# Attention: the scores of two key blocks merged by an elementwise maximum, one transpose per head, the two triangles taken apart on GpSimd

## The chip, the cores and the metric

The kernel runs on one core of a Trainium2 chip. The core has TensorE (matrix products, PE in the profile; PEld is its weight load), VectorE (DVE), ScalarE (ACT), GpSimd (POOL), and SyncE (SP), which here issues DMAs. Each engine works through its own instructions in order and waits on semaphores for the others. The metric is the device time of one execution in microseconds; several runs are taken and their median is given.

## The reference

Three stages follow each other: windowed attention, a mixture of 8 experts of which each row takes one, and a weighted sum over 4 experts.

```
B, H, S, D = q.shape                      # 4, 8, 576, 64
window = 128
scores = scale * np.matmul(q, k.transpose(0, 1, 3, 2))
bias = slopes[:, None, None] * (-np.abs(rel))[None, :, :]     # rel = query - key
mask = (rel >= 0) & (rel < window)
scores = np.where(mask, scores + bias[None], -1000000000.0)
scores = scores - np.max(scores, axis=-1, keepdims=True)
attn = np.exp(scores)
attn = attn / (np.sum(attn, axis=-1, keepdims=True) + 1e-09)
x = np.matmul(attn, v)                    # then [2304, 512]
expert_idx = np.argmax(x @ w_gate, axis=1)
...                                       # each row through relu(x @ w1[e]) @ w2[e] of its expert
...                                       # then sum over 4 experts of p[:, e] * relu(x @ w1[e]) @ w2[e]
```

With a window of 128 a block of 128 queries sees two blocks of 128 keys: its own, where key j counts for query i if j <= i, and the one before, where it counts if j > i. The two triangles complete each other.

## The kernel before

The 2304 rows are 18 tiles of 128. The attention stage is a loop over steps `s`; a step is half a tile (`t, hf = divmod(s, 2)`), that is four heads of 128 queries, so there are 36 steps and some more to empty the pipeline. The order of work on each engine is the order in which the loop writes it; nothing is moved by a scheduler. Each engine keeps that order, so an instruction that waits holds all behind it on its engine.

In step `s` the loop writes, in this order:

- `st_qk(s)`: TensorE puts the bias (two products with an identity, L412) and the scores (12 products in three float32r parts, L420) of both key blocks into PSUM tile `sc`, 128 queries x 4 heads x 256 keys. Two such tiles exist.
- `st_max(s)`: VectorE reduces `sc` to the negated row maximum `nm` (L429).
- `st_exp(s, 0)` and later `st_exp(s, 1)`: ScalarE writes the exponentials, 256 wide, for two heads each, from PSUM into `pr` (L437).
- `st_pv(s - 2)`: TensorE multiplies the transposed probabilities of the step before the last with the values (`xo`, L463; the value tile `vr` also holds a column of ones for the sum and 8 columns of the gate product).
- `st_row(s - 2)`: VectorE normalises (`den`, `xrow`, `lgh`); at the end of a tile it sums the gate logits (`lg`).
- in odd steps `st_vw(t)`: TensorE multiplies the values of the tile with the gate weights (`vw`, L523), and VectorE copies that into `vr`.
- `st_pv_t(s - 1, 0)` and `(s - 1, 1)`: TensorE transposes the probabilities, four 128x128 blocks each (`pt`, L448), and ScalarE copies them out (`ptr`, L450).
- loads (`load`, `load_v`, issued by SP), and the splits of keys and queries into a high and a low part (`split_k`, `split_q`, on VectorE: `khi`, `klo`, `qhi`, `qlo`).
- up to five small pieces of `late_consts` on GpSimd, among them the bias tables (`build_bias`, L302).
- in six of the steps (`SPLITS`) the cast of a weight tile of the expert stage on ScalarE (`whi`, L134), and in the step after it its low half on VectorE (`wlo`, L138).

Four times in a step `route_op` takes one piece of the routing. When the logits of a group of tiles (`CUTS`: four groups of three, two of two, two of one; the last two come after the steps) are there, `st_route` makes the one-hot of the best expert on VectorE (`key`, `km`, `oh_all`), then the rank of each row in its expert on TensorE (`rkp`, L574 to L580), then the row numbers on VectorE (`row_i`, `base`), and GpSimd scatters the rows to HBM with one indirect DMA a tile (L606). After the steps `first_chunk` gathers the first rows of expert 0: those of the first 16 tiles come back from HBM (`early`), those of the last two through products with a placement matrix (`xps`); their casts (L185) begin the expert stage.

Tiles 0 and 9 begin a batch and have one key block; the others have two.

Of the kernel before, what the change touches and what calls it, by code (L numbers as in the profile page):

```python
# [9 lines left out]
F32 = mybir.dt.float32  # L10
F32R = mybir.dt.float32r
BF16 = mybir.dt.bfloat16
I32 = mybir.dt.int32
# [4 lines left out]
P = 128  # L18
# [32 lines left out]
def kernel(  # L51
# [153 lines left out]
    def attention():  # L205
        actx = ExitStack()
        with actx:
# [40 lines left out]
            def split_q(t):  # L248
# [3 lines left out]
                nc.vector.tensor_scalar(out=hi, in0=rq, scalar1=0.125, scalar2=None, op0=ALU.mult)  # L252
# [17 lines left out]
            rel_i = spool.tile([P, 2 * P], I32, tag="pr", name="rel_i")  # L270
# [25 lines left out]
            def build_bias(x, h, o, w, eng):  # L296
                slope = 2.0 ** (-8.0 * (h + 1) / H)
                out = biases[x][:, h, o:o + w]
                if eng is nc.scalar:
                    nc.scalar.activation(out=out, in_=rels[x][:, 0:w], func=AF.Copy, scale=-slope)  # L300
                else:
                    eng.tensor_scalar(out=out, in0=rels[x][:, 0:w], scalar1=-slope, scalar2=None, op0=ALU.mult)  # L302

            for h in range(H):
                build_bias(0, h, 0, 2 * P, nc.scalar)
# [14 lines left out]
            def late_consts():  # L320
                for h in range(H):
                    build_bias(0, h, 2 * P, P, nc.gpsimd)
                    yield

                for x in (1, 2):
# [6 lines left out]
                    for h in range(H):  # L332
                        build_bias(x, h, 0, 2 * P, nc.gpsimd)
                        yield
                        if x == 1:
                            build_bias(x, h, 2 * P, P, nc.gpsimd)
                            yield
                tri = c2.tile([P, P], BF16, tag="tri", name="tri")
                trif = c2.tile([P, P], F32, tag="trif", name="trif")
# [31 lines left out]
                slot_i = c2.tile([P, CH], I32, tag="slot_i", name="slot_i")  # L371
# [61 lines left out]
            def st_exp(s, jj):  # L433
                w = len(geom(s // 2)[0]) * P
                pr, nm = prob[s]
                for r in range(2):
# [923 lines left out]
```

## Time and profile before

| | |
|---|---|
| median of 3 runs | 1180.62 us (1180.06 to 1180.85) |
| the profiled execution, in all | 1181.98 us |
| its span | 1180.3 us |
| mean clock granted to TensorE | 0.995 of full speed |
| TensorE busy | 1161.1 us, 98% of the span |
| VectorE busy | 777.9 us, 66% |
| ScalarE busy | 510.6 us, 43% |
| GpSimd busy | 93.9 us, 8% |

The attention stage is the first 182 us or so. A row of the timeline gives the start in us from the span's start, the time from the first start to the last end, the engine, the line, the operation, the tiles (out<-in), the shape, and how many instructions are merged in it; in square brackets stands how long the engine was idle before, and what it waited for. Matmuls are pipelined, so the distance between two starts counts, not the duration.

### The profile page before, as it was taken

The page shows a single profiled execution, that of the slowest core. Times are in us where ns is not written, and L with a number is a line of the kernel's source. Part 1 is how long each engine was busy: PE and PEld are TensorE (multiplying, and loading weights), DVE is VectorE, ACT ScalarE, POOL GpSimd, SP SyncE. Part 2 cuts the span into 40 slices and gives each one's busy share as a digit, 9 for nine tenths or more (in the row PEclk, how much of TensorE's full clock was granted, in tenths as well). Part 3 has the DMA queues.
Part 4 walks back from the last instruction along what each step waited for, and adds up shares of the span by engine and source line. Part 5 has one row for each costly group of instructions (what it writes and reads, how often), then busy time and mean ns, then how long its engine had stood idle before and what let it go on. Part 6 is the DMA issues. An engine that isn't in the chain of part 4 may idle for free.

```text
span 1180.3 us, 18010 instructions
## 1 busy us (share of the span) xinstructions
PE 1161.1 (98%) x6997; PEld 1060.7 (90%) x6998; DVE 777.9 (66%) x1428; ACT 510.6 (43%) x928; POOL 93.9 (8%) x126
## 2 busy tenths in 40 slices
PE   8999999999999999999999999999999999999997
PEld 6888889999999999999999899999999899999996
DVE  6778865564555476666666976666667866666663
ACT  4565654544454353333334444333334533333331
POOL 8300010002310000000000200000000200000001
PEclk8999999999999999999999999999999999999999
DMA  9856434554564322222112322221221322222201
GB/s 310 272 161 199 135 99 163 167 178 153 174 197 133 116 73 72 72 72 70 56 58 70 116 81 72 72 71 58 70 72 59 120 73 72 72 72 72 72 18 54
DMA packets 62225, 126.60 MB, mean 107 GB/s; under 512 B 26272, under 2 KB 26272, under 8 KB 62112
## 3 DMA queue, kind: packets, MB, share of 16 engines
q1 hardware_dynamic: 58368, 114.96, 30.7%
q0 software_dynamic: 3456, 9.51, 2.1%
q8 instruction: 82, 1.34, 0.4%
q10 hardware_dynamic: 288, 0.52, 0.1%
q14 instruction: 31, 0.25, 0.1%
HBM read 109.18 MB, written 15.80 MB: 106 GB/s over the span
## 4 chain that ended last, share of the span: by engine, by line
issue 70%; PE 25%; DVE 2%; POOL 2%; ACT 0%; DMA 0%; POOLq 0%
PE g L766 6%; PE y L871 6%; PE xo L463 5%; PE sc L420 3%; PE pt L448 2%; POOL out_dram L1291 2%; PE vw L523 1%; PE sc L412 1%; PE xps L838 1%; DMA rk<-in_k_dram 0%; DVE nm L429 0%; DVE xrow L493 0%; DVE qlo L253 0%; DVE qhi L252 0%; PE idle L104 0%
## 5 line engine op out<-in xcount | busy, mean ns | idle before, releaser
L138 DVE TENSOR_TENSOR wlo<-raw,whi 128x1024 fp32r<-128x1024 f32 x160 | 193.3, 1221 | 133.4 <-ACT whi L134 133.4
L1270 PE MATMUL l<-whi,hhi 128*128 128x512 f32 x576 | 224.3, 389 | 1.6 <-DVE acc L1287 1.6
L1270 PE MATMUL l<-whi,hlo 128*128 128x512 f32 x576 | 224.6, 390 | 0.0
L1270 PE MATMUL l<-wlo,hhi 128*128 128x512 f32 x576 | 224.5, 390 | 0.0
L134 ACT CAST whi<-raw 128x1024 fp32r<-128x1024 f32 x160 | 165.9, 1057 | 128.6 <-DVE raw L160 104.6
L1187 ACT COPY x<-X 128x384 f32<-128x384 f32 x126 | 60.6, 481 | 270.0 <-PE X L1166 270.0
L1287 DVE SCALAR_TENSOR_TENSOR acc<-l,ct,acc 128x512 f32<-128x512 f32 x126 | 94.1, 747 | 81.7 <-PE l L1270 81.7
L1270 PEld LDWEIGHTS l<-whi,hhi 128*128 128x128 f32 x576 | 108.1, 188 | 24.3 <-DVE acc L1287 2.5
L1270 PEld LDWEIGHTS l<-whi,hlo 128*128 128x128 f32 x576 | 108.1, 188 | 22.5
L1270 PEld LDWEIGHTS l<-wlo,hhi 128*128 128x128 f32 x576 | 108.1, 188 | 22.0
L1192 DVE TENSOR_TENSOR x<-Z,x 128x384 f32<-128x384 f32 x84 | 44.6, 551 | 67.7 <-ACT x L1187 67.7
L1291 POOL DMA_INDIRECT out_dram<-acc,ctok x18 | 22.3, 1238 | 823.4 <-DVE acc L1287 488.2
L437 ACT ACTIVATE pr<-sc,nm 128x256 f32<-128x256 f32 (+1 forms) x144 | 59.0, 465 | 51.0 <-DVE nm L429 22.5
L1198 ACT ACTIVATE hhi<-x 128x384 fp32r<-128x384 f32 x126 | 58.1, 521 | 30.8 <-DVE x L1192 30.8
L871 PE MATMUL y<-hhi,whi 128*128 128x256 f32 (+2 forms) x224 | 69.5, 310 | 1.6 <-issue 1.6
L463 PE MATMUL xo<-vr,ptr 128*128 128x73 f32 x544 | 69.2, 279 | 0.4 <-ACT ptr L450 0.2
L871 PE MATMUL y<-hhi,wlo 128*128 128x256 f32 (+2 forms) x224 | 69.0, 308 | 0.0
L871 PE MATMUL y<-hlo,whi 128*128 128x256 f32 (+2 forms) x224 | 68.8, 307 | 0.0
L463 PEld LDWEIGHTS xo<-vr,ptr 128*128 128x128 f32 x544 | 63.7, 191 | 5.5 <-ACT ptr L450 0.7
L1204 DVE SCALAR_TENSOR_TENSOR hlo<-x,hhi 128x384 fp32r<-128x384 f32 x126 | 62.8, 552 | 2.7
L755 DVE SCALAR_TENSOR_TENSOR hlo<-g,hhi 128x384 fp32r<-128x384 f32 x64 | 32.7, 552 | 31.0 <-ACT hhi L754 30.9
L754 ACT ACTIVATE hhi<-g 128x384 fp32r<-128x384 f32 x64 | 28.0, 489 | 53.4 <-PE g L852 42.4
(351 smaller groups left out, 2571.4 us busy)
## 6 DMA issues: line engine op xcount, KB each, us to landing
raw<-in_w_b_dram SPq DMA_DIRECT2D x96, 512.0 KB, 3.6
raw<-in_w_a_dram SPq DMA_DIRECT2D x64, 512.0 KB, 4.0
xs<-zrow SPq DMA_DIRECT2D x8, 768.0 KB, 6.3
row<-xs SPq DMA_DIRECT2D x7, 768.0 KB, 5.6
rk<-in_k_dram SPq DMA_DIRECT2D x18, 256.0 KB, 4.2
vr<-in_v_dram SPq DMA_DIRECT2D x18, 256.0 KB, 3.6
rv<-in_vt_dram SPq DMA_DIRECT2D x18, 256.0 KB, 3.5
rq<-in_q_dram SPq DMA_DIRECT2D x16, 256.0 KB, 4.7
```

Source lines behind the costliest of these rows:

```text
L134: nc.scalar.copy(out=hi, in_=src)
L138: nc.vector.tensor_tensor(out=lo, in0=src, in1=hi.bitcast(F32), op=ALU.subtract)
L437: nc.scalar.activation(out=pr[:, r, jj, 0:w], in_=sc[s][:, r, jj, 0:w], func=AF.Exp, bias=nm[:, r, jj:jj + 1], scale=1.0,)
L463: nc.tensor.matmul(xo[:, 2 * jj + r, :], pt[:, r, c, :], vr[:, keys[c] % NSLOT, h, :], start=(c == 0), stop=(c == nk - 1),)
L766: nc.tensor.matmul(ps[:, 0:w], wl[:, c0:c0 + P], xl[dt // 2][:, dt % 2, 0:w], start=(dt == 0 and n == 0), stop=(dt == NDT - 1 and n == 2),)
L871: nc.tensor.matmul(acc[:, 0:w], wl[:, c0:c0 + P], hl[:, 0:w], start=(f == 0 and x == 0), stop=(f == NFT - 1 and x == 2),)
L1187: nc.scalar.copy(out=to, in_=xb[i])
L1198: nc.scalar.activation(out=hi, in_=c, func=AF.Relu)
L1204: nc.vector.scalar_tensor_tensor(out=lo, in0=c, scalar=0.0, in1=hi.bitcast(F32), op0=ALU.max, op1=ALU.subtract)
L1270: nc.tensor.matmul(acc, hl[:, ts], wl[:, c0:c0 + DM], start=(m == 0 and x == 0), stop=(m == 3 and x == 2),)
L1287: nc.vector.scalar_tensor_tensor(out=accs[g], in0=acc, scalar=pe, in1=accs[g], op0=ALU.mult, op1=ALU.add)
L1291: nc.gpsimd.indirect_dma_start(out=outv[g], out_offset=bass.IndirectOffsetOnAxis(ap=ctok[:, g, :], axis=0), in_=accs.pop(g), in_offset=Non ...
```

## The change

Per step and head the two 128-key blocks of scores become one by an elementwise maximum: of each pair one is masked (a very large negative bias), so the maximum keeps the one that counts. ScalarE copies the first block from PSUM to `pr`, VectorE takes the maximum with the second, in place, and reduces it over 128 instead of 256 keys. The exponentials are 128 wide, read and write `pr`, and all four are written together. One transpose per head remains. ScalarE copies the transposed block (`pt`, tile `both`), and GpSimd makes of it two blocks, each with one triangle set to zero (`affine_select`), one for the keys of the same tile and one for those of the tile before. The products with the values stay, two per head, and run three steps behind the scores instead of two, so the loop has one step more. The transposes of step `s - 2` are written behind the scores of step `s` and ahead of the values of step `s - 3`.

With it: from tile 2 on the casts `khi` and `qhi` move from VectorE to ScalarE; the bias tables built inside the steps (32 pieces) move from GpSimd to ScalarE, three a step; `load_v(t + 1)` is issued in the even step `2t` where `load_v(t + 2)` was issued in the odd one, `2t + 1`; two small constants share tiles with others.

```diff
@@ split_k, split_q (the queries alike, with scale=0.125)
-                nc.vector.tensor_copy(out=khi[:, :, c, :], in_=rk)
+                if t < 2:
+                    nc.vector.tensor_copy(out=khi[:, :, c, :], in_=rk)
+                else:
+                    nc.scalar.copy(out=khi[:, :, c, :], in_=rk)
@@ attention
+            def late_biases():
+                for h in range(H):
+                    for o, w in ((0, 2 * P), (2 * P, P)):
+                        build_bias(1, h, o, w)
+                        yield
+                for h in range(H):
+                    build_bias(2, h, 0, 2 * P)
+                    yield
+                for h in range(H):
+                    build_bias(0, h, 2 * P, P)
+                    yield
...
             def st_max(s):
-                w = len(geom(s // 2)[0]) * P
+                scores = sc.pop(s)
+                pr = spool.tile([P, 2, 2, P], F32, tag="pr", name=f"pr{s}", bufs=3)
+                if len(geom(s // 2)[0]) == 2:
+                    nc.scalar.copy(out=pr, in_=scores[:, :, :, 0:P])
+                    nc.vector.tensor_tensor(out=pr, in0=scores[:, :, :, P:], in1=pr, op=ALU.max)
+                    scores = pr
+                else:
+                    scores = scores[:, :, :, 0:P]
                 nm = small.tile([P, 2, 2], F32, tag="nm", name=f"nm{s}")
-                nc.vector.tensor_reduce(out=nm, in_=sc[s][:, :, :, 0:w], axis=AX.X, op=ALU.max, negate=True)
-                pr = spool.tile([P, 2, 2, 2 * P], F32, tag="pr", name=f"pr{s}")
-                prob[s] = pr, nm
+                nc.vector.tensor_reduce(out=nm, in_=scores, axis=AX.X, op=ALU.max, negate=True)
+                prob[s] = pr, nm, scores
...
+            def st_turn(s):
+                keys = geom(s // 2)[0]
+                pr, _, _ = prob.pop(s)
+                ps = ps_t.tile([P, 4, P], F32, tag="t", name=f"pt{s}")
+                for i in range(4):
+                    nc.tensor.transpose(ps[:, i, :], pr[:, i % 2, i // 2, :], ident)
+                both = spool.tile([P, 4, P], F32, tag="pt", name=f"pt{s}")
+                nc.scalar.copy(out=both, in_=ps)
+                if len(keys) == 1:
+                    probt[s] = {s // 2: both}
+                    return
+                probt[s] = {}
+                for d in range(2):
+                    part = spool.tile([P, 4, P], F32, tag=f"pt{d}", name=f"pt{s}_{d}")
+                    nc.gpsimd.affine_select(
+                        out=part, in_=both, pattern=[[0, 4], [1 - 2 * d, P]], base=-d, channel_multiplier=2 * d - 1,
+                        compare_op=ALU.is_ge, fill=0.0,
+                    )
+                    probt[s][s // 2 - d] = part
...
-            for s in range(ns + 2):
+            for s in range(ns + 3):
...
                     st_max(s)
-                    st_exp(s, 0)
+                if 2 <= s < ns + 2:
+                    st_turn(s - 2)
+                if s < ns:
+                    st_exp(s)
                 route_op()
...
-                if 2 <= s < ns + 2:
-                    st_pv(s - 2)
-                    st_row(s - 2)
+                if s >= 3:
+                    st_pv(s - 3)
+                    st_row(s - 3)
...
-                if 1 <= s < ns + 1:
-                    st_pv_t(s - 1, 0)
-                if s < ns:
-                    st_exp(s, 1)
-                if 1 <= s < ns + 1:
-                    st_pv_t(s - 1, 1)
...
-                    for _ in range(5):
-                        if next(consts, True):
-                            pass
+                    for todo in (consts, consts, extra, extra, extra):
+                        next(todo, None)
```

Three places show how the order on the engines changes. The number in a name is that of the step for `sc`, `pr`, `nm`, `xo`, `den` and `pt`, that of the tile for `vw`, `xrow`, `lgh`, `khi`, `qhi`, `rk` (raw keys) and `row`, and that of the group for `rkp`, `key` and `oh_all`; what follows an underscore at the end only numbers the buffers.

First, TensorE at the rank of the group of tiles 9 to 11. Before, in step 26:

```order
L463 MATMUL xo24_1962<-vr_124,ptr24_0_1924 128x73 x4
L463 MATMUL xo24_1962<-vr_124,ptr24_1_1933 128x73 x4
L448 MATMUL pt25_0_1979<-ident_71,pr25_1886 128x128 x4
L448 MATMUL pt25_1_1988<-ident_71,pr25_1886 128x128 x4
L574 MATMUL rkp3_2001<-base_73,top_706 128x32
```

and now, in step 27:

```order
L459 MATMUL pt25_1963<-ident_71,pr25_1827 128x128 x4
L480 MATMUL xo24_1979<-vr_124,pt24_0_1900 128x73
L480 MATMUL xo24_1979<-vr_124,pt24_1_1902 128x73
...
L540 MATMUL vw13_1995<-wbd_195,rv13_1804 128x16 x4
L591 MATMUL rkp3_2006<-base_73,top_280 128x32
```

The transposes, which stood between the values and the rank, now stand ahead of the values, four instead of eight; the gate product `vw13` stands between, since the rank has come into an odd step.

In the same place VectorE, whose `oh_all` the rank needs. Before:

```order
L429 TENSOR_REDUCE nm26_1956<-sc26_1941 128x4
L569 TENSOR_REDUCE km3_1915<-key3_1914 128x3
L488 TENSOR_SCALAR den24_1972<-xo24_1962 128x4
L489 RECIPROCAL den24_1972<-den24_1972 128x4
L493 TENSOR_TENSOR xrow12_1971<-xo24_1962,den24_1972 128x256
L510 TENSOR_TENSOR lgh12_1976<-xo24_1962,den24_1972 128x32
L571 TENSOR_TENSOR oh_all_75<-key3_1914,km3_1915 128x24
```

and now:

```order
L437 TENSOR_TENSOR pr27_1958<-sc27_1943,pr27_1958 128x512
L442 TENSOR_REDUCE nm27_1961<-pr27_1958 128x4
L586 TENSOR_REDUCE km3_1928<-key3_1927 128x3
L505 TENSOR_SCALAR den24_1989<-xo24_1979 128x4
L506 RECIPROCAL den24_1989<-den24_1989 128x4
L510 TENSOR_TENSOR xrow12_1988<-xo24_1979,den24_1989 128x256
L527 TENSOR_TENSOR lgh12_1993<-xo24_1979,den24_1989 128x32
L541 COPY vr_124<-vw13_1995 128x8x8
L588 TENSOR_TENSOR oh_all_75<-key3_1927,km3_1928 128x24
L259 SCALAR_TENSOR_TENSOR qlo15_2003<-rq15_1809,qhi15_2002 128x512
L605 TENSOR_TENSOR rk3_1929<-rkp3_2006,oh_all_75 128x24
L138 TENSOR_TENSOR wlo4_1940<-raw4_1366,whi4_1939 128x1024
```

The one-hot now comes behind the maximum, the reduction and the copy of the gate product, and a query half and a weight half stand around the first routing operation after it.

Second, GpSimd behind the scatter of that group. Before, it held one scatter after another:

```order
L606 DMA xs_69<-xrow9_1568,row_i_76 18433x512
L606 DMA xs_69<-xrow10_1714,row_i_76 18433x512
L606 DMA xs_69<-xrow11_1840,row_i_76 18433x512
L606 DMA xs_69<-xrow12_1971,row_i_76 18433x512
L606 DMA xs_69<-xrow13_2123,row_i_76 18433x512
```

and now:

```order
L468 AFFINE_SELECT pt25_1_1972<-pt25_1968 128x512
L623 DMA xs_69<-xrow9_1589,row_i_76 18433x512
L623 DMA xs_69<-xrow10_1735,row_i_76 18433x512
L623 DMA xs_69<-xrow11_1856,row_i_76 18433x512
L468 AFFINE_SELECT pt26_0_2054<-pt26_2052 128x512
L468 AFFINE_SELECT pt26_1_2056<-pt26_2052 128x512
```

The selections of step 26 now stand behind the three scatters, which wait for VectorE's row numbers.

Third, ScalarE in a step with two key blocks, here step 32. Before:

```order
L437 ACTIVATE pr32_2382<-sc32_2365,nm32_2380 128x256 x2
L450 COPY ptr31_0_2408<-pt31_0_2403 128x512
L437 ACTIVATE pr32_2382<-sc32_2365,nm32_2380 128x256 x2
L450 COPY ptr31_1_2417<-pt31_1_2412 128x512
L437 ACTIVATE pr33_2441<-sc33_2424,nm33_2439 128x256 x2
```

and now:

```order
L436 COPY pr32_2311<-sc32_2296 128x512
L461 COPY pt30_2321<-pt30_2316 128x512
L449 ACTIVATE pr32_2311<-pr32_2311,nm32_2314 128x128 x4
L246 CAST khi_122<-rk17_2084 128x4x128
L196 ACTIVATE sh4_2211<-sh4_2211 128x16
L436 COPY pr33_2372<-sc33_2357 128x512
```

The four exponentials stand together behind two copies, and the cast of the keys comes between them and the copy of the next scores.

## Rows read from the trace of the kernel before

**Rows 1.** Busy time by engine in two stretches, with granted clock (PEclk).

```profile
20.00:176.00 156.00, 154.42 (x1426) 135.60 (x1425) 121.98 (x354) 93.41 (x216) 33.34 (x54) 1.00 0.57 181
8.10:14.40 6.30, 6.04 (x28) 4.13 (x27) 2.86 (x7) 2.93 (x10) 5.91 (x12) 0.50 1.08 376
```

**Rows 2.** Timeline of TensorE: steps 2, 27 to 29 and 35.

```profile
14.37 0.63 PE L412 MATMUL sc<-bias,identb 128*128 128x512 bf16 x1
...
127.25 0.59 PE L412 MATMUL sc<-bias,identb 128*128 128x512 bf16 x2
...
128.68 2.01 PE L463 MATMUL xo<-vr,ptr 128*128 128x73 f32 x16
130.52 1.01 PE L523 MATMUL vw<-wbd,rv 128*128 128x16 f32 x8
131.38 1.07 PE L448 MATMUL pt<-ident,pr 128*128 128x128 f32 x8
132.28 0.59 PE L412 MATMUL sc<-bias,identb 128*128 128x512 bf16 x2
...
136.43 0.59 PE L412 MATMUL sc<-bias,identb 128*128 128x512 bf16 x2
...
164.92 0.59 PE L412 MATMUL sc<-bias,identb 128*128 128x512 bf16 x2
```

**Rows 3.** Timeline of VectorE in steps 26 and 27.

```profile
126.07 0.16 DVE L488 TENSOR_SCALAR den<-xo 128x4 f32<-128x4 f32 x1 [0.55 <-PE xo L463]
...
126.92 0.17 DVE L571 TENSOR_TENSOR oh_all<-key,km 128x24 bf16<-128x24 f32 x1
...
128.86 1.22 DVE L429 TENSOR_REDUCE nm<-sc 128x4 f32<-128x1024 f32 x1 [0.33 <-PE sc L420]
```

**Rows 4.** Timeline of ScalarE: biases, step 0, step 27, end of the drain.

```profile
3.03 2.56 ACT L300 ACTIVATE bias<-rel 128x256 bf16<-128x256 f32 x8
8.17 1.14 ACT L437 ACTIVATE pr<-sc,nm 128x128 f32<-128x128 f32 x4 [2.59 <-DVE nm L429]
...
128.18 1.08 ACT L134 CAST whi<-raw 128x1024 fp32r<-128x1024 f32 x1
130.18 0.84 ACT L437 ACTIVATE pr<-sc,nm 128x256 f32<-128x256 f32 x2 [0.92 <-DVE nm L429]
...
180.50 0.86 ACT L185 CAST x0('s', 0)_0_2751<-xps 128x384 fp32r<-128x384 f32 x2 [1.79 <-PE xps L634]
```

**Rows 5.** ScalarE by line and shape, to 185 us: busy us, mean ns.

```profile
L450 ACT COPY ptr<-pt 128x512 f32<-128x512 f32 x64 | 37.8, 593 | 16.0 <-PE pt L448 15.6
L437 ACT ACTIVATE pr<-sc,nm 128x128 f32<-128x128 f32 x16 | 4.9, 368 | 4.7 <-DVE nm L429 4.7
```

**Rows 6.** VectorE by line and shape, to 185 us.

```profile
L253 DVE SCALAR_TENSOR_TENSOR qlo<-rq,qhi 128x512 fp32r<-128x512 f32 x18 | 12.5, 696 | 0.6
...
L429 DVE TENSOR_REDUCE nm<-sc 128x4 f32<-128x512 f32 x4 | 2.8, 690 | 1.5 <-PE sc L420 1.5
```

**Rows 7.** GpSimd by line and shape.

```profile
L276 POOL TENSOR_SCALAR_AFFINE_SELECT rel<-rel 128x256 f32<-128x256 f32 x2 | 0.8, 400 | 0.1
...
L341 POOL TENSOR_SCALAR_AFFINE_SELECT trif<-trif 128x128 f32<-128x128 f32 x1 | 0.3, 295 | 0.1
```

**Rows 8.** Timeline of GpSimd: scatters of two groups.

```profile
128.74 0.97 POOL L606 DMA_INDIRECT xs<-xrow,row_i  x1 [22.71 <-DVE base L592]
130.01 0.97 POOL L606 DMA_INDIRECT xs<-xrow,row_i  x1 [0.30 <-issue]
...
165.76 0.97 POOL L606 DMA_INDIRECT xs<-xrow,row_i  x1 [15.91 <-DVE base L592]
```

**Rows 9.** Timeline of VectorE and GpSimd where they meet in SBUF.

```profile
19.35 0.69 DVE L244 TENSOR_TENSOR klo<-rk,khi 128x512 fp32r<-128x512 f32 x1
...
19.54 1.22 POOL L302 TENSOR_SCALAR bias<-rel 128x256 bf16<-128x256 f32 x1
...
28.87 1.76 POOL L302 TENSOR_SCALAR bias<-rel 128x256 bf16<-128x256 f32 x2
```

More of the change, by code (lines that the diff above doesn't have):

```diff
@@ L294, in clear_rows, with build_bias @@
                     nc.sync.dma_start(out=xs[E1 * N:E1 * N + 1].rearrange("o (p d) -> (o p) d", d=8), in_=zrow[0:D, 0, 0:8])
-            def build_bias(x, h, o, w, eng):
+            def build_bias(x, h, o, w):
                 slope = 2.0 ** (-8.0 * (h + 1) / H)
[L298 to L302, printed above, removed]
+                nc.scalar.activation(
+                    out=biases[x][:, h, o:o + w], in_=rels[x][:, 0:w], func=AF.Copy, scale=-slope
+                )
             for h in range(H):
-                build_bias(0, h, 0, 2 * P, nc.scalar)
+                build_bias(0, h, 0, 2 * P)
             dpt = c2.tile([P, N // P, E2], F32, tag="dpt", name="dpt")
@@ L331, in late_consts @@
                     yield
[L332 to L337, printed above, removed]
                 tri = c2.tile([P, P], BF16, tag="tri", name="tri")
-                trif = c2.tile([P, P], F32, tag="trif", name="trif")
+                trif = c2.tile([P, P], F32, tag="put16", name="trif")
                 nc.gpsimd.memset(trif, 1.0)
@@ L426, in st_max @@
             def st_max(s):
-                w = len(geom(s // 2)[0]) * P
-                nm = small.tile([P, 2, 2], F32, tag="nm", name=f"nm{s}")
-                nc.vector.tensor_reduce(out=nm, in_=sc[s][:, :, :, 0:w], axis=AX.X, op=ALU.max, negate=True)
-                pr = spool.tile([P, 2, 2, 2 * P], F32, tag="pr", name=f"pr{s}")
-                prob[s] = pr, nm
[L433 to L436, printed above, removed]
-                    nc.scalar.activation(
-                        out=pr[:, r, jj, 0:w], in_=sc[s][:, r, jj, 0:w], func=AF.Exp,
-                        bias=nm[:, r, jj:jj + 1], scale=1.0,
-                    )
@@ L442, in st_pv_t @@
-            def st_pv_t(s, jj):
-                nk = len(geom(s // 2)[0])
-                pr, _ = prob[s]
-                ps = ps_t.tile([P, 2, 2, P], F32, tag="t", name=f"pt{s}_{jj}")
-                for r in range(2):
-                    for c in range(nk):
-                        nc.tensor.transpose(ps[:, r, c, :], pr[:, r, jj, c * P:(c + 1) * P], ident)
-                pt = spool.tile([P, 2, 2, P], F32, tag="pt", name=f"ptr{s}_{jj}", bufs=4)
-                nc.scalar.copy(out=pt[:, :, 0:nk], in_=ps[:, :, 0:nk])
-                probt[s, jj] = pt
+                scores = sc.pop(s)
@@ new lines, in st_max, with st_exp @@
+                prob[s] = pr, nm, scores
+            def st_exp(s):
+                pr, nm, scores = prob[s]
+                for jj in range(2):
+                    for r in range(2):
+                        nc.scalar.activation(
+                            out=pr[:, r, jj, :], in_=scores[:, r, jj, :], func=AF.Exp,
+                            bias=nm[:, r, jj:jj + 1], scale=1.0,
+                        )
+            def st_turn(s):
[15 more added lines that the diff above has]
+                        compare_op=ALU.is_ge, fill=0.0,
+                    )
+                    probt[s][s // 2 - d] = part
@@ L664, in offsets @@
                 nc.vector.tensor_copy(out=off_i, in_=off[0:1])
-            back, late, consts = [], [], late_consts()
+            back, late, consts, extra = [], [], late_consts(), late_biases()
             def route_op():
@@ L696, in attention @@
                     st_vw(t)
[L697 to L698 removed]
+                if hf == 0 and 2 <= t + 1 < NTT:
+                    load_v(t + 1)
                 route_op()
[L700 to L705 removed]
                 if s < ns:
```

36 lines of the change are left out of this document (15 added, 21 removed).

## The prediction

> **What bounds the kernel now.** Read first the busy time of the stretch of the attention steps: between 20 and 176 us TensorE is busy 154.42 of 156 us at the full clock, VectorE 121.98, ScalarE 93.41, GpSimd 33.34 [rows 1]. Read next TensorE's own sequence of one pair of steps [rows 2]: scores 1.43 us (127.25 to 128.68), values 1.84 (to 130.52), the odd step's gate product 0.86 (to 131.38), eight transposes 0.90 (to 132.28), with no gap; the even step has no gate product and takes 4.15. A pair lasts 9.18 us (127.25 to 136.43). Steps 2 to 35 fill 150.55 us (scores of step 2 at 14.37, of step 35 at 164.92). So TensorE sets the pace here, and the other engines wait for it: ScalarE's exponentials stand idle for VectorE's maximum at 130.18, but a step has room for that [rows 4]. Last comes the drain: from the scores of step 35 to the first cast of the expert stage (180.50) are 15.6 us [rows 2, 4].
>
> **TensorE's part of the change.** Four of eight transposes go in each step with two key blocks. Eight take 0.90 us, so four take 0.45; 32 of the 36 steps have two blocks (tiles 0 and 9 have one), which is 32 x 0.45 = 14.4 us. The value products stay (two per head). If nothing else came last, steps 2 to 35 would take 150.55 - 14.4 = 136.2 us, a mean step 4.14 us (9.18 less 0.90, halved).
>
> **ScalarE and VectorE in one step.** Today ScalarE has room. Afterwards one step is a chain that changes engine twice, on two engines that work in order: copy of the first block (as the 128x512 copies, 0.59 [rows 5]), VectorE's maximum (one operand in PSUM, one in SBUF; no row is the same, and nearest are the 128x512 two-operand op at 0.70 and the reduction at 0.69 [rows 6]: I take 0.69), its reduction over half the width (0.69), the hand-over to ScalarE (0.10: the reduction of 128.86 ends at 130.08, the exponential starts at 130.18 [rows 3, 4]; the two hand-overs before it 0 to 0.10, taken as 0.05), four exponentials of half the width (1.14 for four [rows 4]; they will read SBUF and not PSUM, which no row of theirs shows), and the cast of keys or queries that moves over from VectorE (half of the 1.08 weight cast as lower bound, the 0.59 copy as the nearest row: 0.6). That is 3.91; neighbours on ScalarE overlap by 0.11 (four of 0.368 took 1.14, not 1.47 [rows 4, 5]), twice, so 3.7 to 3.9: **3.8 us** against TensorE's 4.14. The copy of the transposes fits into the wait for VectorE. It fits, but hardly, and three things must still go in. 32 bias rows move from GpSimd to ScalarE, three a step; six fall in steps 0 and 1, where ScalarE is idle; of the other 26 half are 256 wide at 0.32 (eight in 2.56 us [rows 4]) and half 128 wide, estimated at 0.20 from the slope between the 0.59 and the 1.08 row: 6.8 us. Six weight casts stay where they were (1.08, less 0.11: 5.8). So ScalarE needs for steps 2 to 35: 32 x 3.8 + 2 x 2.4 (the one-block steps have neither copy nor maximum) + 6.8 + 5.8 = 139.0 us, 2.8 more than TensorE. Bounds: 0, if its lag is taken up by the buffers, to 6.
>
> **The routed groups.** Six groups of tiles are routed inside the steps. Two waits appear at each.
> First the rank product on TensorE. Before, eight transposes stood between the values and it, and its one-hot operand came in that time: the normalisation starts at 126.07 and the one-hot ends at 127.09, 1.02 later [rows 3]. Now the transposes stand ahead of the values, and the gate product (0.86) is what is left as cover; VectorE must do those 1.02 and the copy of the gate product behind maximum and reduction, which end 2.1 us after the scores (0.59 + 0.05 + 0.69 + 0.05 + 0.69) where the one reduction ended after 1.33 (0.11 and 1.22). This is a wait of about 0.4 where ScalarE keeps up, and 1.08 more where a weight cast or the biases stand in front of the copy. I take 0.9 a group.
> Second GpSimd. Its scatter DMAs take 1.27 us each (128.74 to 130.01), three in most groups, and nothing was behind them [rows 8]. Now the two triangle selections of the next step are. A selection of 128x512 isn't in the trace: 0.295 at 128 wide and 0.400 at 256 [rows 7] give 0.61 by the slope, at most 0.80; two are 1.22. From the end of the rank product: one query half on VectorE 0.70, then three small routing ops of some 0.2, GpSimd's start 0.2, scatters 3.8, selections 1.22, in all 6.5; TensorE comes to the values that need them after 1.43 + 0.45 + 1.84 + 1.43 + 0.45 = 5.6 [rows 2]. So 0.9 late, more by 1.2 where a weight's low half falls in between, less in a group of two. I take 1.0 a group. Together 6 x 1.9 = 11.4 us, bounds 3 and 18.
>
> **The drain.** The values come one step later. Behind the last scores stand the copy and the split maximum (0.8 more, as above), the two selections (1.2), and one step's transposes and values that now go ahead (0.45 + 1.84): 4.3. The other way round it comes out alike: the scatter of tiles 14 and 15, which begins at 165.76 [rows 8] and whose rows TensorE needs back before the first chunk, starts a step (4.1) later. I take 4.3, bounds 3 and 6.
>
> Nothing for the rest: the value loads, issued a step later on the same SP queue, still have more than two steps before their use; VectorE loses 0.53 us of the wide reduction and the two casts and gains the maximum; GpSimd is free of the biases.
>
> **Sum:** -14.4 + 2.8 + 11.4 + 4.3 = +4.1 us, against the profiled execution's 1180.3 span and 1181.98 in all. That run lies 1.36 over the median of 1180.62, so the forecast for the median is **1184.7 us**.
>
> **Rivals.** *The waits are absorbed (faster).* TensorE may run a step ahead of ScalarE, since the scores have two banks and the transposes trail by two steps; if the rank and selection waits vanish in that, -14.4 + 2.8 + 4.3 = -7.3 remains: 1173. It decides at 7.3 / 6 = 1.2 us of wait a group. For it: 0.9 of each wait rests on sums of small terms. Against: TensorE, VectorE and GpSimd each wait in order, so one late operand holds all behind it. With waits of 0.8 to 1.6 a group the change is worth nothing.
> *GpSimd slowed by VectorE (slower still).* A 256-wide bias op of GpSimd took 1.22 us at 19.54, beside VectorE's key half from two SBUF operands (19.35, 0.69 long); two at 28.87 took 1.76, so 0.88 each: 0.34 more [rows 9]. If in every two-block step a selection met such a half, GpSimd would be 32 x 0.34 = 11 us longer, about half of it on the path where selections come last: 5 more, 1190. Against it: behind the copy of the transposes VectorE is in maximum and reduction, which don't have two SBUF operands. The Trainium skill states the rule in its GPSIMD Engine Reference, section 8 "Key points": GpSimd shares its SBUF interfaces with VectorE and contends with instructions that run in a two-port mode or read two SBUF inputs. By that rule the two bias times are as they should be, and the trace agrees.
> *The clock falls.* From 8.10 to 14.40 TensorE was granted 0.50 of its clock, the 1.2 GHz level, after stretches of scores with gaps; in the steps it had 1.00 [rows 1]. No wait in those steps is long. If two groups met both waits at once and the clock fell for as long (6.3 us, half of it lost), that is 2 x 3.15 = 6.3 more: 1191.
>
> **Chances.** Waits near those of the sum, 1183 to 1188: 0.42. Waits absorbed: 0.18. Waits about two thirds, no change: 0.20. GpSimd slowed: 0.10. Clock: 0.10. No change is what lies within 0.2% (2.4 us), about what a measurement can tell here. So faster 0.18, same 0.20, slower 0.62. The range is 1175 to 1192: below it lies over half of the absorbed case, above it the worst of the last two, together under 0.2. The likeliest case alone has 1181 to 1189.
>
> **What would show it.** Right: quiet pairs of steps at 8.3 us between scores; idle TensorE before the rank product, put down to VectorE's one-hot, and before the values, put down to GpSimd's selections, the latter behind scatters; scores of step 35 near 165 us in spite of fewer transposes, and the first expert cast near 185. Wrong: scores of step 35 at 153 (waits absorbed), pairs of 9 us without named waits (the ScalarE chain is longer than 3.8), selections far over 0.61, or a granted clock of 0.5 inside the steps. If the drain is no longer than 15.6 us, that term was invented.

## The result and the profile after

The changed kernel takes 1195.38 us (median of six runs, 1192.83 to 1200.73), the kernel before 1181.15 on the same chips: 1.0125 times as long, interval 1.010 to 1.015. The forecast was slower, 1184.7, with a range up to 1192. The sign is right; the size is 10.7 us short, and the result lies outside the range.

First the busy times in the same stretch as [rows 1], and then in the stretches where the profile has TensorE's granted clock at 0.50 (columns as there; the last row is their sum, without clock and DMA):

```profile
20.00:176.00 156.00, 145.47 (x1212) 123.15 (x1211) 110.42 (x324) 102.48 (x263) 51.69 (x73) 0.89 0.53 173
...
44.48:51.30 6.82, 6.82 (x35) 5.76 (x36) 5.27 (x13) 5.47 (x16) 1.23 (x2) 0.50 0.75 219
54.72:58.13 3.41, 3.41 (x21) 2.46 (x18) 1.24 (x5) 1.04 (x4) 1.86 (x2) 0.50 0.16 59
82.03:92.27 10.24, 9.95 (x55) 7.86 (x56) 4.69 (x18) 5.06 (x12) 4.18 (x5) 0.50 0.30 102
112.75:116.16 3.41, 3.41 (x23) 2.35 (x24) 1.04 (x4) 1.94 (x4) 1.11 (x2) 0.50 1.03 383
140.05:150.29 10.24, 9.94 (x55) 7.85 (x56) 5.74 (x19) 4.24 (x11) 4.18 (x5) 0.50 0.37 131
184.43:194.66 10.23, 10.23 (x50) 10.14 (x50) 4.78 (x23) 0.81 (x2) 1.63 (x3) 0.50 0.30 103
sum 44.35, PE 43.76 PEld 36.41 DVE 22.75 ACT 18.56 POOL 14.19; mean PE 7.29 PEld 6.07 DVE 3.79 ACT 3.09 POOL 2.36
```

Before, the steps had 1.00 throughout. Now TensorE runs at the 1.2 GHz level in five stretches inside the steps (34.1 us) and in one in the drain, and there it is busy 43.76 of 44.35 us: it isn't waiting, it is slow. Next TensorE's timeline: a quiet pair of steps, then what stood ahead of the falls, the last step, and the drain.

```profile
64.30 0.59 PE L418 MATMUL sc<-bias,identb 128*128 128x512 bf16 x2
...
72.49 0.59 PE L418 MATMUL sc<-bias,identb 128*128 128x512 bf16 x2
...
44.37 3.56 PE L480 MATMUL xo<-vr,pt 128*128 128x73 f32 x16 [1.66 <-DVE vr L541]
...
82.32 0.61 PE L591 MATMUL rkp<-base,top 128*128 128x32 f32 x2 [1.49 <-DVE lgh L527]
...
112.67 0.53 PE L591 MATMUL rkp<-base,top 128*128 128x32 f32 x2 [2.34 <-DVE lgh L527]
...
140.35 0.61 PE L591 MATMUL rkp<-base,top 128*128 128x32 f32 x2 [1.67 <-DVE lgh L527]
...
174.33 0.59 PE L418 MATMUL sc<-bias,identb 128*128 128x512 bf16 x2
...
180.03 1.90 PE L480 MATMUL xo<-vr,pt 128*128 128x73 f32 x16
...
183.39 3.45 PE L480 MATMUL xo<-vr,pt 128*128 128x73 f32 x16 [1.01 <-POOL pt L468]
```

The quiet pair takes 8.19 us where it took 9.18 [rows 2]: what was to be gained is there. Four of the five falls inside the steps begin inside a long wait of TensorE or 0.1 us behind it: three before a rank product, one (44.48) before values that wait for VectorE's copy of the gate product. The fifth (54.72) follows a wait of 0.27, 3.4 us after the first stretch ended. Sixteen value products then take 3.45 to 3.56 us instead of 1.90; step 16, which lies wholly in such a stretch, lasts 6.75 (82.87 to 89.62) instead of 3.67. The scores of step 35 come at 174.33 (before 164.92), and the first cast of the experts, the end of the drain, at 197.20 (180.50 [rows 4]):

```profile
197.20 0.86 ACT L185 CAST x0('s', 0)_0_2707<-xps 128x384 fp32r<-128x384 f32 x2 [3.00 <-PE xps L651]
```

### The profile page after: what moved, and what is told of

Read it like the earlier page. It is cut to its first block, busy times and chain, and to the rows that moved or that the text cites. A ratio compares the mean times of both kernels' runs of the same rounds, so it can differ in the third digit from the quotient of the medians.

```text
span 1194.9 us, 17899 instructions
## 1 busy us (share of the span) xinstructions
PE 1168.6 (98%) x6870; PEld 1063.3 (89%) x6870; DVE 773.0 (65%) x1428; ACT 525.4 (44%) x988; POOL 110.2 (9%) x158
## 3 DMA queue, kind: packets, MB, share of 16 engines
q8 instruction: 81, 1.33, 0.5%
## 4 chain that ended last, share of the span: by engine, by line
issue 69%; PE 21%; DVE 3%; ACT 3%; POOL 2%; DMA 1%; POOLq 0%; SPq 0%; ACTq 0%; DVEq 0%
PE g L779 6%; PE y L884 6%; PE xo L480 3%; PE sc L426 2%; POOL out_dram L1304 2%; ACT pr L449 1%; PE pt L459 1%; PE sc L418 1%; DVE nm L442 1%; DVE pr L437 1%; PE xps L851 1%; PE vw L540 1%; ACT pr L436 0%; DMA xs<-zrow 0%; DVE klo L247 0%
## 5 line engine op out<-in xcount | busy, mean ns | idle before, releaser
L480 PE MATMUL xo<-vr,pt 128*128 128x73 f32 x544 | 73.9, 293 | 5.4 <-DVE vr L541 3.7
L480 PEld LDWEIGHTS xo<-vr,pt 128*128 128x128 f32 x544 | 71.7, 211 | 7.0 <-POOL pt L468 4.9
L449 ACT ACTIVATE pr<-pr,nm 128x128 f32<-128x128 f32 x128 | 40.9, 390 | 35.6 <-DVE nm L442 35.2
```

The source lines that it names most:

```text
L449: nc.scalar.activation(out=pr[:, r, jj, :], in_=scores[:, r, jj, :], func=AF.Exp, bias=nm[:, r, jj:jj + 1], scale=1.0,)
L480: nc.tensor.matmul(xo[:, i, :], pt[c][:, i, :], vr[:, c % NSLOT, 4 * hf + i, :], start=(n == 0), stop=(n == len(pt) - 1),)
```

## The experiments

Three theories. Theory 1: TensorE's waits at the routed groups let its granted clock fall, and the falls are most of what the forecast lacks. Theory 2: the falls cost nothing; ScalarE's chain, with the casts and bias rows that it was given, sets the pace (in c2 the loads of ScalarE and VectorE, in c3 the wait alone). Theory 3: the longer pipeline and its drain. Below, "steps 12 to 35" is the time between the scores of those two steps in the profiled run: 105.04 us before, 110.03 after. A profile shows one execution; where that one lies far from the median of its kernel, it is said.

**Dummies where TensorE waits.** `a1_fill_rank` has six dummy products ahead of each rank product; `a2_fill_both` has four more ahead of the values that follow a group's scatters.

```
+                if t0 < 16:
+                    busy(ps_t, "t", 6)
                 pr = ps_m.tile([P, m + 1, E1], F32, tag="m", name=f"rkp{g}")
...
+                while fills:                  # a2 alone: 4, set by st_route
+                    busy(ps_t, "t", fills.pop())
                 if s >= 3:
                     st_pv(s - 3)
```

> The changed kernel with six dummy products (128x512, bf16, into a bank that nobody reads) on TensorE ahead of the rank product of six groups; nothing is left out. Theory 1 (clock): about 10 us of the result are the granted clock at 0.5, and the waits are only what lets it fall. Three of the five falls inside the steps (82.03, 112.75, 140.05) begin within 0.4 us of a rank product that had waited 1.49, 2.34 and 1.67 us; the steps from there on are 2.2, 3.1 and 1.2, then 2.1, then 2.4, 3.1 and 1.2 us longer than the quiet steps of 3.67 and 4.52, together 15.3, of which the three waits are 5.5. If TensorE works through those waits, the granted clock stays 1.00 there, and the time falls by 15.3 - 5.5 = 9.8, less what the dummies cost beyond the waits (6 x 0.26 = 1.56 each by the two bias products' 0.52, so 0 to 3 in all): 1186 to 1189, although work was added. The fall at 44.48, which follows a wait for the selections, stays. Theory 2 (the waits and the ScalarE/VectorE chain are the whole loss, the low clock costs nothing because TensorE waits anyway): nothing gained, 1195 to 1199.

> As the kernel with dummies ahead of the rank products, and four more dummies ahead of the values that follow a group's scatters, where TensorE waits for the selections; nothing is left out. Theory 1: no fall inside the steps and none in the drain (there 184.43 to 194.66 now, after a wait of 1.01 for the selections); all five falls inside the steps gone gives about 22.5 us of excess less 7.5 us of waits = 15 back, less 3 to 9 for dummies that nothing hides: 1184 to 1190. Against the other kernel of this pair it shows whether the falls after the selections cost more than four dummies (1.0) a group. Theory 2: 1198 to 1205, six times 1.0 on top.

Measured: 1216.31 (1.0316 times before, 1.029 to 1.034) and 1196.12 (1.014, 1.011 to 1.017). Neither theory had either number; a1 is 17 us over both. Its profiled run is 17.5 us longer than that of the changed kernel (spans 1212.5 and 1194.9), and 10.6 of that are there at the scores of step 35 (184.91). In a1 the rank product of the fourth group no longer waits, but then the values wait 1.62 us for the selections, and the clock falls there, for 23.89 us in which TensorE is busy all the time:

```profile
149.22 3.85 PE L480 MATMUL xo<-vr,pt 128*128 128x73 f32 x16 [1.62 <-POOL pt L468]
...
149.73:173.62 23.89, 23.81 (x113) 19.39 (x113) 9.56 (x33) 8.65 (x20) 3.79 (x8) 0.50 0.17 57
```

In a2, where both waits are filled, the second group can be laid beside that of the changed kernel: both reach step 15's scores at about the same time (76.20 and 76.16).

```profile
80.73 1.46 PE L104 MATMUL idle<-idle 128*128 128x512 bf16 x6
82.37 0.38 PE L593 MATMUL rkp<-base,top 128*128 128x32 f32 x2 [0.19 <-DVE lgh L527]
...
84.61 1.03 PE L104 MATMUL idle<-idle 128*128 128x512 bf16 x4
85.48 1.90 PE L480 MATMUL xo<-vr,pt 128*128 128x73 f32 x16
...
91.77 0.38 PE L418 MATMUL sc<-bias,identb 128*128 128x256 bf16 x2
```

The clock stays at 1.00, and the scores that come at 91.77 here came at 95.30: with 2.5 us more work, these steps take 3.6 us less. That is the clock's price at one group. A wait alone doesn't always bring a fall: the third group's rank product still waits 1.45 in a2 (109.55), and the clock falls only at 119.59, 2.7 us behind a wait of 0.60. Over the whole, a2 has 10.2 us of half clock in the steps instead of 34.1, and the experts' first cast comes 4.9 us earlier (192.27). The time doesn't show it, since the expert stage then begins later: in a1 and a2 alone TensorE's sequencer holds its first product for 4.9 us (1.3 to 1.5 in the others), and the clock falls again there.

```profile
197.47 0.66 PE L785 MATMUL g<-x0('s', 0)_0_2779,whi 128*128 128x384 f32 x1 [4.88 <-PEq L914]
```

For 3.70 us of it (192.45 to 196.15) the sequencer stands in the branch ahead of the stage, which takes 0.36 in the changed kernel. A 16 KB transfer of instructions starts inside that time (193.11), as in a1 (208.73, in a branch from 207.78 to 211.54); that the branch waits for it is not shown.

**The causes of the waits, one at a time.** `a3_late_rank` issues the rank product two routing turns later; `a4_casts_back` has the casts of keys and queries on VectorE again; `b4_no_late_bias` leaves out the bias rows made inside the steps (those steps use the rows made ahead of step 0).

```
                 nc.vector.tensor_tensor(out=oh, in0=key, in1=km.to_broadcast([P, m, E1]), op=ALU.is_equal)
                 yield
+                if t0 < 12:                   # a3
+                    for _ in range(2):
+                        yield
...
-                    nc.scalar.copy(out=khi[:, :, c, :], in_=rk)       # a4; qhi alike
+                    nc.vector.tensor_copy(out=khi[:, :, c, :], in_=rk)
...
-            back, late, consts, extra = [], [], late_consts(), late_biases()   # b4
+            back, late, consts, extra = [], [], late_consts(), iter(())
```

> The changed kernel with the rank product of the groups of tiles 0 to 13 issued two routing turns later (half a step), so that the one-hot has that long to come; nothing is left out. Theory 1: the rank product no longer waits (1.49, 2.34, 1.67 and more before), the falls that follow it don't come, 15 us less at most; falls after the selections may stay: 1180 to 1186. Theory 2 (ScalarE and VectorE set the pace of the steps whatever TensorE waits for): the wait moves to the next operand, 1192 to 1196.

> The changed kernel with the casts of keys and queries on VectorE again, as before the change; nothing is left out. ScalarE is rid of 31 x 0.61 = 18.9 us, VectorE has 31 x about 0.5 more. Theory 2 (ScalarE's chain sets the pace): a good part of 18.9 comes back, 1178 to 1186, also in steps without a group. Theory 1: the quiet pairs (8.19 us) are TensorE's already and stay as they are; the waits at the groups get shorter by up to 0.6 each where the copy of the transposes stood behind a cast, the falls of the clock mostly stay: 1188 to 1194.

> The changed kernel without the 32 bias rows that ScalarE makes inside the steps; it leaves out this part of the computation, and all steps use the rows made ahead of step 0. The prediction has them at 6.8 us of ScalarE's time, of which 2.8 on the path. The profile after has 26 of them between 20 and 176 us, 403 and 295 ns each, 9.1 us. Theory 1: they only matter to the first steps (2 to 12), where the fall at 44.48 may go too: 2 to 7 less, 1188 to 1194. Theory 2 (ScalarE's chain is the bound): 8 to 10 less, 1185 to 1187, with the same granted clock.

Measured: 1191.15 (runs from 1184.05 to 1197.59), 1196.88 and 1193.67. a3 lies between the theories. Its profiled run is the fastest of the four (1184.05): of its rank waits 0.93 and 1.02 are left, and values behind the first wait 1.47. The 1.02 is at the fifth group, tiles 12 and 13, which the edit (`t0 < 12`) leaves alone although the expectation names them. a4 is outside of both theories: ScalarE has some 19 us less to do and nothing is gained. The rank waits of its first five groups add up to 7.4 us instead of 6.3; the first one's goes from 0.27 to 2.21, the fourth's from 1.67 to 0.74:

```profile
49.97 0.60 PE L585 MATMUL rkp<-base,top 128*128 128x32 f32 x2 [2.21 <-DVE vr L535]
...
80.73 0.60 PE L585 MATMUL rkp<-base,top 128*128 128x32 f32 x2 [1.22 <-DVE lgh L521]
...
111.30 0.61 PE L585 MATMUL rkp<-base,top 128*128 128x32 f32 x2 [2.55 <-DVE lgh L521]
...
146.65 2.50 PE L474 MATMUL xo<-vr,pt 128*128 128x73 f32 x16 [1.36 <-POOL pt L462]
```

b4, which theory 1 has, is 1.7 us under the changed kernel by the medians, within the scatter of its runs (1190.68 to 1199.15): the wait at 44.37 and its fall are gone, but the rank products wait 2.86, 1.46 and 2.74 instead. Taking work off ScalarE alone brings next to nothing; theory 2 falls as the whole cause.

**All causes together.** `b1_rank_scatter_casts` has the later rank product, the casts back on VectorE, and a routing turn between a group's scatters; `b2_rank_scatter` the same without the casts; `c2_rank_casts` without the space between scatters.

```
                 for j, t in enumerate(tiles):
+                    if j and t0 < 12:
+                        for _ in range(1):
+                            yield
                     nc.gpsimd.indirect_dma_start(
```

> The changed kernel with three edits: the rank product of the groups of tiles 0 to 11 two routing turns later, their scatters one a routing turn instead of three in a row, and the casts of keys and queries on VectorE again; nothing is left out. Theory 1 (waits over 1 us on TensorE let the granted clock fall, and the falls are most of the loss): with the rank waits and the selections' waits gone inside the steps no fall is left there; the steps come near to the quiet pairs of 8.19 us, 17 x 8.19 less half a pair = 134.7, with 8 to 14 us left for the first steps, the routing and the waits under 1 us: scores of step 35 near 158 to 163, time 1174 to 1182. Theory 2 (ScalarE's chain sets the pace): the casts alone brought nothing (1196.9), so with them no more than the later rank product (1191): 1188 to 1193.

> The later rank product and the scatters one a routing turn, with the casts on ScalarE as in the changed kernel; nothing is left out. Theory 1: both kinds of wait shrink, falls are fewer than with the later rank product alone (four inside the steps there): 1178 to 1188. Theory 2: as with the later rank product alone, 1189 to 1193. Against the kernel with the casts moved back it gives the price of the casts on ScalarE where no group waits: I expect 2 to 6 us.

> The kernel of the three edits with the scatters three in a row again (later rank product and casts on VectorE only); nothing is left out. Theory 1 (waits, then the clock): after groups the selections stand behind up to 3.9 us of scatters again, values wait 0.7 to 1.6 us, and one to three falls come back inside the steps: 1178 to 1186. Theory 2 (two engines' loads: the casts off ScalarE and the rank product out of VectorE's way are what counts): as with all three, 1175 to 1178.

Measured: 1175.75 (0.996, 0.9946 to 0.9974), 1187.89 (1.0054, 1.0035 to 1.0074) and 1181.36 (0.9996, 0.998 to 1.001). Theory 1 has all three, b2 at the edge of its range and close to theory 2's 1189, so that b2 doesn't tell the two apart. In b1's profile the longest wait inside the steps is 0.95 us, no step runs at half clock, and steps 12 to 35 take 97.67 us. (This run has the highest granted clock of b1's five, 0.994 against 0.988 to 0.992, and yet is the longest: its step 2 begins at 14.44, in c1 at 10.82. Where the clock fell in the other four was not recorded.) A row as at the top, of most of its steps:

```profile
56.00:160.00 104.00, 100.82 (x937) 86.51 (x936) 96.04 (x281) 61.92 (x157) 46.08 (x60) 1.00 0.55 171
```

It beats both kernels. c2, in its profiled run (the fastest of ten, at the highest clock), has one wait of 1.62 at the fifth group's rank product, one fall behind it (142.43 to 145.84), and steps 12 to 35 in 100.98. I had the casts at 2 to 6 us in b2; they are 12, and in part by something theory 1 doesn't have. The clock falls at 88.08, though TensorE was busy until then:

```profile
87.52 3.85 PE L480 MATMUL xo<-vr,pt 128*128 128x73 f32 x16 [0.15 <-DVE sh L194]
...
80.00:88.08 8.08, 7.81 (x73) 6.58 (x72) 6.07 (x20) 5.95 (x15) 5.37 (x7) 1.00 0.69 177
88.08:98.00 9.92, 9.90 (x51) 9.37 (x52) 5.71 (x15) 4.51 (x14) 3.51 (x4) 0.50 0.59 205
98.00:108.56 10.56, 10.56 (x55) 8.44 (x56) 5.04 (x17) 2.96 (x7) 0.00 (x0) 0.50 0.08 19
```

**One wait put back.** `c3_one_rank_early` is b1 with the rank product of tiles 6 to 8 at its earlier place.

```
-                if t0 < 12:
+                if t0 in (0, 3, 9):
                     for _ in range(2):
                         yield
```

> The kernel of the three edits with one group's rank product, that of tiles 6 to 8, at its earlier place again; nothing is left out. There it waited 2.55 us in the kernel with the casts back (until 111.30), where it waits 0.61 (until 101.60) with the three edits. Theory 1: at this one place a wait of 2 to 2.6 and a fall of the granted clock to 0.5 that lasts some steps; scores of step 35 (155.44) come by the longer wait, 1.9, and by 2 to 5 for the fall: 159 to 162, time 1178 to 1183. Theory 2 (the wait is the whole cost and the low clock is free): 1.9 more at most, scores of step 35 by 157.4, time 1175.5 to 1178.

Measured: 1178.86 (0.9981, 0.9971 to 0.9991), 3.1 more than b1. The wait and one fall are there, and at no other place in the steps beyond the start (12.89 to 19.72):

```profile
99.11 0.61 PE L588 MATMUL rkp<-base,top 128*128 128x32 f32 x2 [2.55 <-DVE lgh L521]
...
98.22:105.05 6.83, 5.94 (x33) 4.72 (x34) 3.77 (x13) 3.87 (x10) 1.97 (x3) 0.50 0.75 268
```

Steps 12 to 35 take 100.61, 2.94 more than in b1. The longer wait is 1.94 of it (2.55 less 0.61), so this fall costs 1.0 net; two waits that b1 has behind this place, 0.95 and 0.48, are gone in c3, so the slow clock took up time that TensorE would have waited. The scores of step 35 come at 155.80, where theory 1 had 159 to 162 and theory 2 up to 157.4; the time is in theory 1's range and 0.9 above theory 2's. It shows that a wait brings a fall here and what that costs; it is too small to tell the theories apart by time alone.

**The longer pipeline and its drain.** `b3_short` has the values two steps behind the scores again. `c1_rows_behind` is b1 with the early rows' first transposes behind the last values; `c4_rows_biases` has that and the bias rows spread otherwise.

```
-                if 2 <= s < ns + 2:            # b3
-                    st_turn(s - 2)
...
-                if s >= 3:
-                    st_pv(s - 3)
+                if s >= 2:
+                    st_pv(s - 2)
...
+                if 1 <= s < ns + 1:
+                    st_turn(s - 1)
...
                     st_pv(s - 3)               # c1, c4
+                    if s == ns + 2:
+                        first_rows(0)
...
-   for todo in (consts, consts, extra, extra, extra):                 # c4
+   for todo in (consts, consts, *[extra] * (4 if s < 2 else 2)):
```

> The changed kernel with the values two steps behind the scores again, as before the change, and the transposes of a step behind the values of the one ahead; nothing is left out. Between the transposes and the values that need their selections stand then only the next scores, 1.43 us, where the copy (0.58), two selections (1.23) and three hand-overs need at least 2.0, and the copy may stand behind a cast (0.6). Theory 1 (waits on TensorE, then the clock): a wait of 0.6 or more in nearly every step, 20 us or more, and half clock in large parts of the steps besides: 1205 to 1235. Theory 3 (the longer pipeline and its drain are what the change lost by): 4 to 7 back, 1188 to 1191.

> The kernel of the three edits (later rank product, spaced scatters, casts on VectorE; 1175.75), with the first four transposes of the early rows behind the last step's values instead of ahead of them; nothing is left out. In its drain TensorE waits 1.78 us for these rows (until 168.85), and the values behind them need nothing of it. If that wait is on the path that ends the drain: 1.8 less, and the values (16 in 3.53 us at the low clock there) run while the rows come, 1172 to 1175; if the fall of the clock in the drain (167.17 to 177.41) goes with it, up to 4 more, 1169 to 1171. Rival: the drain is set by VectorE's and GpSimd's chain behind the values of tile 16 and 17, not by this wait: 1175 to 1177.

> The kernel of the three edits with the early rows' first transposes behind the last values, and the bias rows spread otherwise: eight narrow ones ahead of step 0, four a step in steps 0 and 1 and two a step after, instead of three a step; nothing is left out. With the three edits the steps 3 to 13 still last 4.47 to 4.61 us where 3.66 would do in each second of them; three bias rows are about 1.05 us of ScalarE (403 and 295 ns each), so two are 0.35 less a step for nine steps: 3 less than the kernel with the early rows behind alone, 1168 to 1173. Rival: VectorE, which has the casts again, sets these steps: no less than that kernel.

Measured: 1247.28 (1.0573, 1.0547 to 1.0598), 1176.09 and 1173.95 (0.9942, 0.9925 to 0.9959). b3 is 12 us over theory 1's range, and 56 over theory 3's: the shorter pipeline gives nothing back. Without the longer one the values wait some 0.6 us for the selections in step after step, and the granted clock averages 0.78 and 0.66:

```profile
60.00:120.00 60.00, 53.98 (x373) 45.52 (x372) 34.79 (x96) 29.96 (x77) 21.30 (x25) 0.78 0.43 131
120.00:180.00 60.00, 56.72 (x344) 47.64 (x343) 32.76 (x98) 28.00 (x67) 17.58 (x20) 0.66 0.40 120
```

What the drain costs by itself b3 doesn't show.

In c1 the rival is right: the wait for the rows goes, 0.75 us stand before the last values instead, and nothing is gained. c4 is the fastest kernel of the study, 2.1 us under c1 (the intervals overlap) and 0.95 above what was expected at most. What its profiled run gained lies in steps 2 to 11 (42.60 us, 44.70 in c1). Only 0.6 of it is at step 8, which goes from 4.62 to 4.00; 1.4 is at steps 2 to 5, where c1's clock falls (13.12 to 19.95) and that of c4, after nearly the same wait, doesn't. So the gain by the bias rows is not shown beyond step 8. Steps 10 and 12 still last 4.49 and 4.53, so bias rows weren't what made those long. VectorE is busy there 29.86 of 33.40 us (20.00 to 53.40).

## Why the prediction was wrong

By its own steps:

- *TensorE's part*: right. The quiet pair was put at 8.3 us and is 8.19.
- *ScalarE and VectorE in one step*: the durations hold, by line and shape (20 to 176 us):

```profile
L449 ACT ACTIVATE pr<-pr,nm 128x128 f32<-128x128 f32 x124 | 39.6, 390 | 34.7 <-DVE nm L442 34.3 <-issue 0.4
...
L246 ACT CAST khi<-rk 128x512 fp32r<-128x512 f32 x16 | 9.7, 604 | 0.0
...
L304 ACT ACTIVATE bias<-rel 128x256 bf16<-128x256 f32 x13 | 4.8, 403 | 0.0
L304 ACT ACTIVATE bias<-rel 128x128 bf16<-128x128 f32 x13 | 3.4, 295 | 0.0
...
L437 DVE TENSOR_TENSOR pr<-sc,pr 128x512 f32<-128x512 f32 x30 | 20.7, 689 | 17.2 <-ACT pr L436 15.2 <-issue 1.9
...
L468 POOL TENSOR_SCALAR_AFFINE_SELECT pt<-pt 128x512 f32<-128x512 f32 x58 | 37.8, 677 | 82.5 <-ACT pt L461 79.9 <-PE xo L480 2.7
```

  The maximum is 0.689 (0.69 forecast), the cast 0.604 (0.6), a selection 0.677 (0.61), an exponential from SBUF 390 ns (368). The bias rows were under-sized, 8.2 us for these 26 instead of 6.8.
- *The routed groups*: their sum is right by luck. Between 20 and 176 us TensorE waits 10.5 us, where 11.4 were put. But the wait for the selections, put at 1.0 a group, comes last only once with more than 0.2 us there, 0.26 (at 28.46); a1 shows that it stands behind the rank wait (1.62 at the fourth group once that is filled). In its place came a wait that was not forecast, 1.50, 0.59 and 1.66 for VectorE's copy of the gate product, behind a maximum that waits for ScalarE's copy (25.19, 34.20 and 44.37; the expectations above still called the last a wait for the selections). The rank wait was put at 0.9 a group; it is 0.27, 1.49, 2.34, 1.67, 0.51 and 0.27, so 1.1 in the mean, with the releaser that was named. The high end (0.4 + 1.08) was reserved for weight casts and biases, but at the second group, for one, ScalarE's four exponentials (77.11) and the key cast (78.29) stand in front of the copy (78.80).
- *The drain*: 4.3 forecast; 22.87 - 15.58 = 7.3 measured. In a2, whose drain has no fall, it is 192.27 - 171.78 = 20.5, so 4.9 (with four dummies in it); the rest is put down to the clock.
- *The clock* is the step that failed: "No wait in those steps is long. If two groups met both waits at once and the clock fell for as long (6.3 us, half of it lost) ...", a rival at 0.10, and nothing in the sum. The forecast had a rank wait of 0.4 to 1.5 us at every group in its own sum, and didn't ask of each what the clock would do. It fell at five places inside the steps, 34.1 us in all, and in the drain; half clock inside the steps is one of the signs of being wrong that the prediction names.

The price can be read from the six runs of the changed kernel, the same program at different clocks: spans from 1191.6 us at a mean granted clock of 0.984 to 1198.9 at 0.974. Mean clock lost, doubled, times the span is the time at half clock: 38 and 62 us, so 7.3 us for 24, or 0.30 a us. (A line through all six gives 0.32, one through the ten runs of c2 0.24, those of c1 and c4 0.11 and 0.14, and the runs of b1 and c3 show none: it is an estimate, and for this kernel.) The changed kernel's profiled run has some 48 us at half clock (0.980), that of before some 12 (0.995): 36 x 0.30 = 11 us, where 10.7 were missing. The Trainium skill ("TensorE: Matmul & The Clock Gate", section "Terms") puts the penalty at about the throttled time times the share of pulses withheld, a half; an estimate by that rule is 18 us here. The runs show less; that TensorE would have waited for part of it anyway is seen in c3 alone.

So: the sum without the clock, +4.1, was about right, in part by luck, and the clock's 11 us (estimated) were priced at nothing. From the scores of step 2 to those of step 35 the changed kernel takes 159.9 us, where TensorE's own work was put at 136.2: of the 23.7 between them 10.5 are waits and about 10 the clock (34.1 x 0.30), which leaves some 3 for ScalarE's 2.8. What let it fall is shown as far as this: four of five falls inside the steps begin at a wait of 1.5 to 2.3 us; with those waits gone (the profiles of b1, c1, c4) none is left behind step 3, and one put back (c3) brings one. A wait neither suffices nor is it the only way. The wait of 1.50 at 25.19 brought no fall, the fall at 88.08 in b2 had no wait ahead, and those at 29.32 in a3 and 30.06 in b2 none over 0.3 us in the 5 us before. In step 2 nearly the same wait went with a fall in c3 (first row; 12.89 to 19.72, and the product after it takes 0.58 us) and without one in c4 (second row, 0.38 us):

```profile
13.61 0.58 PE L420 MATMUL sc<-khi,qhi 64*128 64x256 f32 x2 [2.30 <-DVE qhi L252]
...
13.72 0.38 PE L418 MATMUL sc<-khi,qhi 64*128 64x256 f32 x2 [2.32 <-DVE qhi L252]
```

What decides between the two, and what sets a fall's length (3.4 to 23.9 us), is open. The drain's fall is gone in a2 alone; b1, c1 and c4 still have it.

## What to carry to other kernels

Where one engine at full clock sets the pace, a wait that a change creates on it has two prices, the wait and the clock behind it: here the waits, the five falls and the drain gave back twice the 14.4 us that four transposes a step had gained. Price each wait of the sum for the clock as well. And look for the next wait behind the one that is cut: with the rank waits filled, the values' wait brought the fall (a1), and of the kernels run here only those with the later rank product, the spaced scatters and the casts together (in c3 for all groups but one) beat the kernel before, at 1173.95 with two edits more.

## What was not expected of the hardware

The granted clock stays at 0.50 for 10 to 24 us while TensorE is busy 97 to 100% of it (82.03 to 92.27; 149.73 to 173.62 in a1, both shown above). The Trainium skill ("TensorE: Matmul & The Clock Gate", section "Seeing it yourself") warns that the trace's records of the clock can be unreliable; here the durations agree with them, 3.5 us for sixteen value products at 0.50 and 1.90 at 1.00.

GpSimd's selections slow some VectorE ops beside them: with four selections running from 182.67 to 185.07, the three-operand 128x8 op took 1.08 us, and 0.23 at 192.80 without them. In b1 three query scalings (`qhi`, 128x512) took 0.98 to 1.00 us wholly beside selections, and eleven without them 0.42. The reduction to the maximum (0.69) and the sum column read from PSUM (`den`, 0.16) took the same with and without.

```profile
183.44 1.08 DVE L578 SCALAR_TENSOR_TENSOR key<-lgl,mxl,kc 128x8 f32<-128x8 f32 x1
...
192.80 0.23 DVE L578 SCALAR_TENSOR_TENSOR key<-lgl,mxl,kc 128x8 f32<-128x8 f32 x1
```

The forecast's rival had it the other way round, GpSimd slowed by VectorE. That is there as well, and more than the 0.34 a meeting that was put: of the 58 selections between 20 and 176 us, four that ran beside VectorE's weight halves (`wlo`, at 71.04, 97.84, 120.92 and 169.07) took 1.01 to 1.33 us, the other 54 took 0.64 on the average. The rival put such a meeting in every two-block step; four meetings are 2 us, so that part is small.
